# Order of loads, stores, first weight sums and last stores around the two ends of a mixing and routing kernel

## Chip, cores and metric

One core of a Trainium2 chip runs the whole kernel. The metric is the device time of one execution in microseconds (us), as the median of several runs. The engines are TensorE (PE, matmuls), VectorE (DVE), ScalarE (ACT), GpSimd (POOL) and SyncE (SP). Each has its own instruction stream; SP, ACT and POOL also issue DMAs, each on its own queue, in the order of the stream. An instruction that must wait holds up all that stands behind it in the same stream.

## The reference

```python
# x: 8 batches of 2496 tokens with 256 channels; 8 experts, F = 1024
X = np.fft.rfft(x, axis=1)                     # along the tokens
y = np.fft.irfft(X * (filt_r + 1j * filt_i), n=x.shape[1], axis=1)
x = y.reshape(8 * 2496, 256)
expert_idx = token_ids * np.int64(2654435761) % np.int64(8)
for e in range(8):
    mask = expert_idx == e
    h = np.maximum(x[mask] @ w1[e], 0.0)
    out[mask] = h @ w2[e]
```

All is float32. First the tokens of a batch are mixed by a filter in the frequency domain, then each mixed row goes through the two layers of the expert that its token's hash names.

## The kernel before

**Mixing.** The transform over 2496 = 39 x 64 tokens is done by matmuls with small tables in stages: stage 1 (`pa`), a turn or a trip through DRAM, forward (`pb`, then the filter's products `y` and `z` on DVE), back (`pc`), a second turn or trip, and stage 3 (`pd`), whose result `o` is copied out of PSUM. Batches 0 and 1 (`first`, `second`) are done on the chip alone, in the head, with transposes on PE between the stages. Batches 2 to 7 go through DRAM: stage 1 writes `mid` to d (batch 2's such stores are collected in a list, `put_off`, and issued together later), `load2` reads `mid` back, `load4` reads `t` back after the second trip. `load1` loads x, in three parts v = 0, 1, 2.

**Sorting.** In the head, the hashes of all tokens are counted on PE, DVE and POOL (`count`, `route`, `later`), which gives each token its row in a DRAM array `xs` that is sorted by expert into tiles of 256 tokens. POOL scatters every mixed row there by indirect DMA (L413): 44 scatters for batches 0 and 1.

**Experts.** 85 tiles are laid out; 80 always run, and up to 5 more in three nested conditional blocks at the end, by a count that is read at run time. With these inputs no conditional block is entered. A tile i loads its rows (`load`: four parts `xg` and a part `no` with the rows' numbers, L799), has them transposed (`token_parts`, DVE, L810), and multiplies by w1 (`up`, L842) and w2 (`down`, L877). Both layers of a tile use one level of Strassen's scheme: sums of the tile's blocks (`token_sums`, DVE, `st`, L823) and of the weights' blocks (`weight_sums`, `tw`, L832: four subtractions of 128x512, each of two SBUF operands) save products. `weight_sums(0)` runs on DVE, those of later tiles on POOL, one tile ahead. Tiles from 50 on use a second form (`both`) for both layers. `store` (L970) scatters the two halves of a tile's output rows `osb` to the output by indirect DMA on POOL. `weights(i + 2, k)` loads w1 or w2 of the tile after next on SP's queue.

**What sets the order.** A list `todo` holds pairs of a time and a piece of work. Pieces with a negative time run before tile 0, in the order of their times. The others are merged into the tiles: `run_until(t)` issues all with a time below t, and within tile i it is called before `down` with i + .6, in `down` after each of the first three quarters with i + .7, i + .8 and i + .9, and after `down` with i + 1. `spaced(a, b, n)` gives n times from a to b. So the stages of batches 2 to 7 are woven into the tiles, and each engine executes its part of this one order. Tiles are in stages by the batches whose rows they need: tiles 0 to 9 hold rows of batches 0 and 1 alone, and `load(10)` needs batch 2's too.

**Around the change.** The lines are those of the kernel before.

- Head, SP's queue: the first batch's x, the tables of part 1 (`load_tables(1)`: a part of the d-table and of the filter), then the second batch's x (`second.load1`, v = 0, 1, 2), each behind other tables (L470 to L486, L238).
- `begin()` (time -84.9) closes the pools of the head, opens those of the tiles (`gath`, `work`, `outs`, `nums`, `tpool`) and issues `load(0)` and `load(1)`, all ten parts on SP's queue. They wait for the last scatter of batch 1.
- Behind them on SP's queue: batch 3's x, parts 0 and 1 (times -75.3, -75.2), and batch 2's `mid` (`load2`, -75 to -74.7). On ACT's queue: the `put_off` stores (-75.5; L749).
- After the pieces, `token_parts(0)`, `token_sums(0)` and `weight_sums(0, nc.vector)` stand in this order on DVE; POOL's `weight_sums(1)` is the first of tile 0's step.
- `part2(2, ...)` and `part3(2, ...)` give the times of batch 2's forward, back and stage 3 and of their loads: the first `pb` is due at .5, in tile 0.
- At the end, after tile 79: `store(79)`, then `token_parts` of tiles 80 to 84 into spare parts of `mid`, and `load(82)` to `load(84)` on ACT's queue, then the conditional blocks (`rest`).

Of the kernel before, what the change touches and what calls it, by code (L numbers as in the profile page):

```python
# [11 lines left out]
F32 = mybir.dt.float32  # L12
# [7 lines left out]
P = 128  # L20
B, S, C = 8, 2496, 256
# [98 lines left out]
def kernel(  # L120
# [55 lines left out]
    def slot(kind):  # L176
# [8 lines left out]
                   for k in range(2)],  # L185
            "st": [spare[:, FP * C + 512 * k:FP * C + 512 * k + 512].rearrange("p (k t) -> p k t", k=4)
                   for k in range(2, 4)],
            "one": spare[:, FP * C + 2048:FP * C + 2048 + P]}

    def minus(eng, out_, a, b, op=OP.subtract):  # L190
        eng.tensor_tensor(out_, a, b, op=op)
# [278 lines left out]
    def load_tables(part):  # L470
        if part < 2:

            nc.gpsimd.tensor_copy(junk[:], first.x[2 * part][0:1, 0, 0:1])
        sl = S_PARTS[part]
        nc.sync.dma_start(out=d_t[:, sl, :], in_=d_dram.ap()[:, sl, :])
        for k in range(2):
            load_filter(k, sl)
# [250 lines left out]
                step(batches[j // (NS // 2)], j % (NS // 2))  # L728


    todo = [(t, lambda k=k: load_tables(k)) for k, t in enumerate((-160, -159, -157, -156))]
    todo += [(t, lambda v=v: second.load1(v)) for v, t in enumerate((-158, -156.5, -156.4))]
    todo += [(t, lambda u=u: first.stage1_c(u)) for u, t in enumerate(spaced(-155, -151, NU))]
    todo += [(-154.2, count), (-152, route), (-150.9, later)]
    todo += [(-137.2, places), (-128, tile_experts), (-121, experts), (-90, blanks)]
# [10 lines left out]
    todo += [(t, lambda v=v: batches[2].load1(v)) for v, t in enumerate((-119, -117.5, -116))]  # L746
    todo += [(t, lambda u=u: batches[2].stage1(u)) for u, t in enumerate((-101.5, -99.5, -84.8, -84.7, -84.6, -84.5))]

    todo += [(-75.5, lambda: [nc.scalar.dma_start(out=dram, in_=chip) for dram, chip in put_off])]  # L749
    todo += [(t, lambda k=k: weights(k // 2, k % 2)) for k, t in enumerate((-101, -98, -95, -92))]  # L750
    todo += [(-84.9, lambda: begin())]

    def batch(b, t1, t2, t3):

# [6 lines left out]
        return out  # L761

    todo += [(-75 + .1 * g, lambda g=g: batches[2].load2(g)) for g in range(4)]
    todo += [(-75.3 + .1 * v, lambda v=v: batches[3].load1(v)) for v in range(2)]
    todo += part2(2, spaced(.5, 3, N_2), [None] * 4 + [1], .6)
    todo += part3(2, spaced(4.3, 7.3, NU), [3.4, 3.6, 4.5]) + part1(3, spaced(1, 4, NU), [None, None, 2])
    todo += part2(3, spaced(6.4, 10, N_2), [5.2, 5.4, 5.6, 6.5, 7.5], .6)
    todo += part3(3, spaced(12, 16, NU), [11.2, 11.4, 12.5])
    todo += batch(4, (7.5, 11), (12.4, 16.4), (18.3, 22.3)) + batch(5, (13, 17), (18.4, 21.6), (23.2, 26.8))
# [6 lines left out]
    main = [t for t in todo if t[0] >= 0]  # L776


    gath = work = outs = nums = tpool = None
    xg, to_rows, parts, sums, rows = {}, {}, {}, {}, {}  # L780

    def begin():
        nonlocal gath, work, outs, nums, tpool
        rctx.close()
        gath, work, outs = pool(ctx, "gath", 2), pool(ctx, "work", 1), pool(ctx, "outs", 2)
        nums, tpool = pool(ctx, "nums", 8), pool(ctx, "tp", 2)
        for i in range(2):
            load(i)

    def load(i):  # L790

        g = gath.tile([P, TB // 32, C // 4], F32, name=f"xg_{i}", tag="xg")
        no = nums.tile([P, 2], I32, name=f"no_{i}", tag="no")
        rows = xs[tiles[i] * TB:(tiles[i] + 1) * TB, :]
        moves = [(g[32 * q:32 * q + 32, :, :], rows[:, 64 * q:64 * q + 64].rearrange("(a t) c -> t a c", t=32))
                 for q in range(4)]
        moves.append((no[:].bitcast(F32), rows[:, C:C + 1].rearrange("(h p) c -> p (h c)", p=P)))
        for to, src in moves:
            ld = (nc.sync if i < 2 else nc.scalar).dma_start(out=to, in_=src)  # L799
            for b in range(STAGES[stage_of[i]], B):  # L800
                tc.declare_no_dep(ld.ins, group=f"xs_{b}", reason="the tiles of a stage hold tokens of its batches alone")
            if stage_of[i] < G - 1:
                tc.declare_no_dep(ld.ins, group="xs_pad", reason="places without a token lie in the last stage alone")
            tc.add_to_no_dep_group("xs_read", ld.ins)
        xg[i], to_rows[i] = g, no
# [78 lines left out]
    def both(i, ht):  # L884

        w1, w2 = ws[i][0:2]
        x, st, t = parts[i], parts[i]["sums"], sums[i]
        t2, s, one = late["t2"][i % 2], late["sums"], late["one"]
        h11, h12, h21, h22 = [ht[:, h, 4 * f:4 * f + 4, :] for h in range(2) for f in range(2)]
        b11, b12, b21, b22 = [w2[:, 4 * f:4 * f + 4, P * c:P * c + P] for f in range(2) for c in range(2)]  # L890
        half = F // 2

        def bank(k, name):
            p, tag = (banks[k], k) if k in banks else (fps, "f")
            return p.tile([P, 4, P], F32, name=f"{name}_{i}", tag=tag)

        def product(ps, w, xx, first):
            for f in range(4):
                nc.tensor.matmul(out=ps[:, f, :], lhsT=w[:, f * P:(f + 1) * P], rhs=xx,  # L899
                                 start=first and f == 0, stop=True, skip_group_check=True)  # L900

        def second(ps, a, b, first):
            for f in range(4):
                nc.tensor.matmul(out=ps[:, 0, :], lhsT=a[:, f, :], rhs=b[:, f, :],  # L904
                                 start=first and f == 0, stop=True, skip_group_check=True)

        def relu(out, in_):
            nc.scalar.activation(out=out, in_=in_, func=AF.Relu)  # L908

        def plus(out, ps, other):  # L910
            nc.vector.tensor_tensor(out, ps, other, op=OP.add)  # L911

        a, b, c = [bank(k, "up" + k) for k in "abc"]
        g, e = bank("f", "upg"), bank("f", "upe")
        if i + 1 < NSURE:
            token_parts(i + 1, late["xt"][i % 2])
        product(a, w1[:, 0, 0:half], x[0, 0], True)
        nc.scalar.copy(out=h21, in_=a[:])
        if i + 2 < NT:
            load(i + 2)  # L920
        product(b, t[1], st[:, 1, :], True)
        plus(h12, b[:], h21)
        product(g, t[2], st[:, 2, :], True)
        plus(h21, g[:], h12)
        product(c, t[0], st[:, 0, :], True)
        plus(h22, c[:], h21)
        relu(h22, h22)
        product(e, t[3], x[1, 1], True)
        plus(h21, e[:], h21)
        relu(h21, h21)  # L930
        product(a, w1[:, 1, 0:half], x[0, 1], False)
        relu(h11, a[:])
        minus(nc.vector, s[:, 0], h21, h22, OP.add)
        product(c, w1[:, 1, half:], st[:, 3, :], False)
        plus(h12, c[:], h12)
        relu(h12, h12)
        weights(i + 2, 0)

        e, a = bank("b", "dne"), bank("d", "dna")
        b, c = bank("f", "dnb"), bank("f", "dnc")  # L940
        rows[i] = outs.tile([P, 2, C], F32, name=f"osb_{i}", tag="osb")
        o11, o12, o21, o22 = [rows[i][:, h, P * k:P * k + P] for h in range(2) for k in range(2)]
        second(e, h22, t2[:, 3], True)
        second(c, s[:, 0], t2[:, 0], True)
        second(a, h11, b11, True)
        nc.scalar.copy(out=one, in_=a[:, 0, :])
        minus(nc.vector, s[:, 1], s[:, 0], h11)
        minus(nc.vector, s[:, 2], h11, h21)
        minus(nc.vector, s[:, 3], h12, s[:, 1])
        second(b, s[:, 1], t2[:, 1], True)  # L950
        if i + 1 < NSURE:
            token_sums(i + 1, late["st"][i % 2], range(2))
        plus(o22, c[:, 0, :], one)
        plus(o21, e[:, 0, :], one)
        plus(o12, b[:, 0, :], one)
        second(a, h12, b21, False)
        nc.scalar.copy(out=o11, in_=a[:, 0, :])
        if i + 1 < NSURE:
            token_sums(i + 1, None, range(2, 4))
        second(b, s[:, 2], t2[:, 2], False)  # L960
        plus(o22, b[:, 0, :], o22)
        plus(o21, b[:, 0, :], o21)
        second(c, s[:, 3], b22, False)
        plus(o12, c[:, 0, :], o12)
        weights(i + 2, 1)
# [11 lines left out]
        piece()  # L977
    token_parts(0)
    token_sums(0)
    weight_sums(0, nc.vector)  # L980
    used = []

    def run_until(t):
# [32 lines left out]
            used.append(nc.values_load(used_i[0:1, 0:1], min_val=0, max_val=NT))  # L1016
        step(i)
    assert not main
    store(NSURE - 1)

    for i in range(NSURE, NT):
        token_parts(i, mid[:, i - NSURE, 0:2 * TB].rearrange("p (d h t) -> p d h t", d=DP, h=2))
        if i + 2 < NT:
            load(i + 2)
    blocks = [range(NSURE, NSURE + 1), range(NSURE + 1, NSURE + 2), range(NSURE + 2, NT)]

    def rest(k):
        with tc.If(used[0] > blocks[k][0]):
            for i in blocks[k]:
                ht = work.tile([P, 2, FP, P], F32, name=f"ht_{i}", tag="ht")  # L1030
                token_sums(i)
                weight_sums(i, nc.vector)
                up(i, ht)
                weights(i + 2, 0)
                down(i, ht)
                store(i)
                weights(i + 2, 1)
            if k + 1 < len(blocks):
                rest(k + 1)

    rest(0)

# [1 line left out]
_INS = ['x', 'filt_r', 'filt_i', 'moe_token_ids', 'moe_w1', 'moe_w2']  # L1044
# [24 lines left out]
```

## Time and profile before

| what | us |
|---|---|
| median of 3 runs (1466.46 to 1475.76) | 1469.89 |
| the profiled execution | 1478.73 |
| its span (first to last recorded event) | 1477.0 |
| PE busy in it | 1386.2 |
| DVE busy | 890.2 |
| POOL busy | 822.2 |
| ACT busy | 417.0 |
| HBM read and written over the span | 254 GB/s |

The profile is taken of one execution, whose time lies 8.84 us above the median. A line of the timeline gives the start, the busy time, the engine (PEld is the load of a matmul's stationary operand, SPq and ACTq are DMAs that the engine issues), the line of the kernel, the operation, `out<-in` by the program's names and how many of them follow each other without a break; in brackets stands the idle time of the engine before them and what ended it. In the page's second part the span is cut into 40 equal slices of 36.9 us, and a digit is the busy share in tenths.

| stretch | from, to (us) | what runs |
|---|---|---|
| head, first batch's x under way | 0 to 8.39 | tables, ids; PE idle |
| head, batches 0 and 1 and batch 2's stage 1 | 8.39 to 138.8 | PE, DVE and ACT mixing; scatters from 79.27 |
| seam | 138.8 to 154.7 | last scatters, batch 2's stores, first rows |
| tile 0 | 154.72 to 180.95 | first products, two `pb` groups |
| tiles 1 to 79 | 180.95 to 1463.7 | experts, batches 2 to 7 among them |
| end | 1463.7 to 1477.0 | last store, loads and transposes for tiles 80 to 84 |

### The profile page before, as it was taken

The page shows a single profiled execution, that of the slowest core. Times are in us where ns is not written, and L with a number is a line of the kernel's source. Part 1 is how long each engine was busy: PE and PEld are TensorE (multiplying, and loading weights), DVE is VectorE, ACT ScalarE, POOL GpSimd, SP SyncE. Part 2 cuts the span into 40 slices and gives each one's busy share as a digit, 9 for nine tenths or more (in the row PEclk, how much of TensorE's full clock was granted, in tenths as well). Part 3 has the DMA queues.
Part 4 walks back from the last instruction along what each step waited for, and adds up shares of the span by engine and source line. Part 5 has one row for each costly group of instructions (what it writes and reads, how often), then busy time and mean ns, then how long its engine had stood idle before and what let it go on. Part 6 is the DMA issues. An engine that isn't in the chain of part 4 may idle for free.

```text
span 1477.0 us, 26433 instructions
## 1 busy us (share of the span) xinstructions
PE 1386.2 (94%) x9466; PEld 1285.2 (87%) x9466; DVE 890.2 (60%) x1644; ACT 417.0 (28%) x770; POOL 822.2 (56%) x732
## 2 busy tenths in 40 slices
PE   6996699989999979999989999999999999999996
PEld 6984688879988868888978999999999999999996
DVE  6872466366465547534754468744656677777775
ACT  3553032223223213323222322222222222222221
POOL 5065323663475456558533487878855555555552
PEclk9999699999999989999999999999999999999998
DMA  8248466756897597688754667597751616161612
GB/s 218 56 131 251 144 196 186 215 167 208 260 272 232 182 279 247 193 272 274 256 155 130 193 212 249 182 268 240 232 183 45 213 44 211 44 211 41 209 41 55
DMA packets 245027, 273.10 MB, mean 185 GB/s; under 512 B 129020, under 2 KB 214959, under 8 KB 235469
## 3 DMA queue, kind: packets, MB, share of 16 engines
q1 hardware_dynamic: 87991, 168.19, 35.9%
q10 hardware_dynamic: 136982, 58.59, 16.0%
q0 software_dynamic: 19920, 44.59, 8.7%
q8 instruction: 77, 1.26, 0.3%
q14 instruction: 57, 0.47, 0.1%
HBM read 291.03 MB, written 83.53 MB: 254 GB/s over the span
## 4 chain that ended last, share of the span: by engine, by line
PE 59%; DMA 8%; DVE 1%; ACTq 1%; ACT 1%; issue 1%; SPq 0%; DVEq 0%
PE dps L877 16%; PE up_b L842 5%; PE dnc L904 4%; PE dna L904 4%; PE dnb L904 4%; DMA t<-d 3%; PE upa L899 3%; PE upc L899 3%; PE up_a L842 3%; DMA xg<-xs 3%; PE up_c L842 3%; PE pd L256 2%; PE pc L323 2%; PE pb L300 2%; PE upe L899 2%; PE upg L899 2%
## 5 line engine op out<-in xcount | busy, mean ns | idle before, releaser
L877 PE MATMUL dps<-wts,ht 128*128 128x256 f32 x1600 | 378.5, 388 | 27.6 <-ACT ht L846 27.6
L877 PEld LDWEIGHTS dps<-wts,ht 128*128 128x128 f32 x1600 | 307.2, 194 | 76.9 <-ACT ht L846 32.5
L970 POOL DMA_INDIRECT out_dram<-osb,no x160 | 167.1, 1044 | 261.9 <-DVE osb L911 142.8
L413 POOL DMA_INDIRECT xs<-o,sidx x176 | 176.5, 1003 | 175.1 <-issue 73.6
L832 POOL TENSOR_TENSOR tw<-wts 128x512 f32<-128x512 f32 x158 | 203.7, 1290 | 109.6 <-DMA wts<-in_moe_w_dram 79.4
L832 POOL TENSOR_TENSOR tw<-wts,tw 128x512 f32<-128x512 f32 x158 | 205.8, 1302 | 6.2
L849 DVE TENSOR_TENSOR ht<-up_b,ht 128x512 f32<-128x512 f32 x150 | 103.7, 691 | 112.0 <-PE up_b L842 102.3
L846 ACT ACTIVATE ht<-ht 128x512 f32<-128x512 f32 x150 | 92.0, 627 | 233.2 <-DMA xg<-xs 92.5
L310 DVE TENSOR_TENSOR z<-pb,filt 64x512 f32<-64x512 f32 x160 | 110.2, 689 | 36.4 <-PE pc L323 34.5
L842 PE MATMUL up_a<-xt,wts 128*128 128x128 f32 x800 | 115.6, 278 | 16.1 <-DVE xt L810 16.1
L882 DVE COPY osb<-dps 128x512 f32<-128x512 f32 x50 | 34.6, 692 | 155.0 <-PE dps L877 154.4
L842 PEld LDWEIGHTS up_a<-xt,wts 128*128 128x128 f32 x800 | 106.3, 194 | 19.6 <-POOL tw L832 16.5
L842 PE MATMUL up_b<-st,tw 128*128 128x128 f32 x800 | 107.6, 278 | 3.1 <-DVE ht L849 1.4
L842 PEld LDWEIGHTS up_b<-st,tw 128*128 128x128 f32 x800 | 98.5, 194 | 4.6 <-issue 2.5
L306 DVE TENSOR_TENSOR y<-pb,filt 128x512 f32<-128x512 f32 x80 | 55.2, 690 | 67.7 <-PE pb L300 65.8
L849 DVE TENSOR_TENSOR ht<-up_c,ht 128x512 f32<-128x512 f32 x100 | 69.1, 691 | 38.8 <-PE up_c L842 33.4
L908 ACT ACTIVATE ht<-ht 128x512 f32<-128x512 f32 x90 | 56.8, 631 | 121.4 <-DVE ht L911 76.0
L853 ACT COPY ht<-up_a 128x512 f32<-128x512 f32 x50 | 29.3, 586 | 175.4 <-PE up_a L842 160.1
L256 PE MATMUL pd<-t,wi_t 120*117 120x256 f32 x320 | 76.1, 380 | 1.3 <-DVE t L386 1.3
L326 ACT COPY mid<-pc 128x512 f32<-128x512 f32 x60 | 35.1, 585 | 146.5 <-PE pc L323 146.4
L311 DVE TENSOR_TENSOR y<-y,z 128x512 f32<-128x512 f32 x80 | 72.5, 907 | 2.7
L258 ACT COPY o<-pd 117x512 f32<-117x512 f32 x80 | 45.5, 586 | 99.3 <-PE pd L256 76.6
(203 smaller groups left out, 2482.1 us busy)
## 6 DMA issues: line engine op xcount, KB each, us to landing
wts<-in_moe_w_dram SPq DMA_DIRECT2D x160, 1024.0 KB
xg<-xs ACTq DMA_DIRECT2D x332, 64.0 KB
mid<-d SPq DMA_DIRECT2D x60, 256.0 KB
d<-mid ACTq DMA_DIRECT2D x60, 256.0 KB
d_t<-t2s SPq DMA_DIRECT2D x15, 1024.0 KB
e_t<-t2s SPq DMA_DIRECT2D x15, 1024.0 KB
d<-mid ACTq DMA_DIRECT2D x12, 960.0 KB
t<-d SPq DMA_DIRECT2D x12, 960.0 KB
```

Source lines behind the costliest of these rows:

```text
L256: nc.tensor.matmul(out=ps[0:cols * H, k, :], lhsT=w[:], rhs=src[:, 2 * i + k, :], start=True, stop=True)
L310: nc.vector.tensor_tensor(out=z[b], in0=ps[a], in1=f_t[1][64 * hi:64 * hi + 64, s1:s1 + 2, :], op=OP.mult)
L311: nc.vector.tensor_tensor(out=y[:], in0=y[:], in1=z[:], op=OP.add)
L413: st = nc.gpsimd.indirect_dma_start(out=xs[:], out_offset=bass.IndirectOffsetOnAxis(ap=index, axis=0), in_=rows, in_offset=None, bounds_ch ...
L832: eng.tensor_tensor(t[k][:], p, q, op=OP.subtract)
L842: nc.tensor.matmul(out=ps[bank][:, f, :], lhsT=w[:, f * P:(f + 1) * P], rhs=xx, start=first and f == 0, stop=True, skip_group_check=True)
L846: nc.scalar.activation(out=out, in_=in_, func=AF.Relu)
L849: nc.vector.tensor_tensor(out, ps[bank][:], other, op=OP.add)
L877: nc.tensor.matmul(out=ps[:, h, :], lhsT=ht[:, h, fp, :], rhs=w2[:, fp, :], start=(fp == 0), stop=(fp == FP - 1))
L899: nc.tensor.matmul(out=ps[:, f, :], lhsT=w[:, f * P:(f + 1) * P], rhs=xx, start=first and f == 0, stop=True, skip_group_check=True)
L904: nc.tensor.matmul(out=ps[:, 0, :], lhsT=a[:, f, :], rhs=b[:, f, :], start=first and f == 0, stop=True, skip_group_check=True)
L970: st = nc.gpsimd.indirect_dma_start(out=out[:], out_offset=bass.IndirectOffsetOnAxis(ap=to_rows[i][:, h:h + 1], axis=0), in_=o[:, h, :], i ...
```

## The change

Several edits stand in one diff. In the head: 14 matmuls of the identity with itself into a PSUM tile that nothing reads (`warm`); the first part of the second batch's x goes ahead of `load_tables(1)`; the `put_off` stores go from ACT's queue to SP's, where they stand behind the row loads and ahead of `load2`, and batch 3's x goes behind `load2`; `load(0)` and `load(1)` leave `begin` for a piece of their own, and of tile 0's five parts the last two are issued on ACT's queue; the pools of the tiles are opened in another order, and `weight_sums(0)` on DVE is issued in `begin`, ahead of tile 0's transpose. In the tiles: batch 2's forward, back and stage 3 get later times (the first `pb` at 1 instead of .5, the first `pd` at 4.6 instead of 4.3) and their loads too. At the end: tile 79's output rows get a buffer of their own in an idle part of the filter's tile (`late["last"]`), only tiles 80 and 81 are transposed ahead of the conditional blocks, the loads and transposes of tiles 82 to 84 move into the third block, and tile 79's store is issued behind the blocks, its second half first.

```diff
--- before.py
+++ after.py
@@ -185,7 +185,8 @@
                    for k in range(2)],
             "st": [spare[:, FP * C + 512 * k:FP * C + 512 * k + 512].rearrange("p (k t) -> p k t", k=4)
                    for k in range(2, 4)],
-            "one": spare[:, FP * C + 2048:FP * C + 2048 + P]}
+            "one": spare[:, FP * C + 2048:FP * C + 2048 + P],
+            "last": spare[:, FP * C + 2048 + P:FP * C + 2048 + P + 2 * C].rearrange("p (h c) -> p h c", h=2)}
 
     def minus(eng, out_, a, b, op=OP.subtract):
         eng.tensor_tensor(out_, a, b, op=op)
@@ -728,8 +729,15 @@
                 step(batches[j // (NS // 2)], j % (NS // 2))
 
 
-    todo = [(t, lambda k=k: load_tables(k)) for k, t in enumerate((-160, -159, -157, -156))]
-    todo += [(t, lambda v=v: second.load1(v)) for v, t in enumerate((-158, -156.5, -156.4))]
+    def warm(n):
+
+        ps = banks["a"].tile([P, 4, P], F32, name="warm", tag="a")
+        for k in range(n):
+            nc.tensor.matmul(out=ps[:, k % 4, :], lhsT=ident[:], rhs=ident[:], start=True, stop=True)
+
+    todo = [(-165, lambda: warm(14))]
+    todo += [(t, lambda k=k: load_tables(k)) for k, t in enumerate((-160, -159, -157, -156))]
+    todo += [(t, lambda v=v: second.load1(v)) for v, t in enumerate((-159.5, -156.5, -156.4))]
     todo += [(t, lambda u=u: first.stage1_c(u)) for u, t in enumerate(spaced(-155, -151, NU))]
     todo += [(-154.2, count), (-152, route), (-150.9, later)]
     todo += [(-137.2, places), (-128, tile_experts), (-121, experts), (-90, blanks)]
@@ -746,9 +754,9 @@
     todo += [(t, lambda v=v: batches[2].load1(v)) for v, t in enumerate((-119, -117.5, -116))]
     todo += [(t, lambda u=u: batches[2].stage1(u)) for u, t in enumerate((-101.5, -99.5, -84.8, -84.7, -84.6, -84.5))]
 
-    todo += [(-75.5, lambda: [nc.scalar.dma_start(out=dram, in_=chip) for dram, chip in put_off])]
+    todo += [(-75.5, lambda: [nc.sync.dma_start(out=dram, in_=chip) for dram, chip in put_off])]
     todo += [(t, lambda k=k: weights(k // 2, k % 2)) for k, t in enumerate((-101, -98, -95, -92))]
-    todo += [(-84.9, lambda: begin())]
+    todo += [(-84.9, lambda: begin()), (-84.4, lambda: [load(i) for i in range(2)])]
 
     def batch(b, t1, t2, t3):
 
@@ -761,9 +769,9 @@
         return out
 
     todo += [(-75 + .1 * g, lambda g=g: batches[2].load2(g)) for g in range(4)]
-    todo += [(-75.3 + .1 * v, lambda v=v: batches[3].load1(v)) for v in range(2)]
-    todo += part2(2, spaced(.5, 3, N_2), [None] * 4 + [1], .6)
-    todo += part3(2, spaced(4.3, 7.3, NU), [3.4, 3.6, 4.5]) + part1(3, spaced(1, 4, NU), [None, None, 2])
+    todo += [(-74.5 + .1 * v, lambda v=v: batches[3].load1(v)) for v in range(2)]
+    todo += part2(2, spaced(1, 3.5, N_2), [None] * 4 + [1.5], .6)
+    todo += part3(2, spaced(4.6, 7.5, NU), [4.0, 4.1, 4.8]) + part1(3, spaced(1, 4, NU), [None, None, 2])
     todo += part2(3, spaced(6.4, 10, N_2), [5.2, 5.4, 5.6, 6.5, 7.5], .6)
     todo += part3(3, spaced(12, 16, NU), [11.2, 11.4, 12.5])
     todo += batch(4, (7.5, 11), (12.4, 16.4), (18.3, 22.3)) + batch(5, (13, 17), (18.4, 21.6), (23.2, 26.8))
@@ -776,16 +784,16 @@
     main = [t for t in todo if t[0] >= 0]
 
 
+    sums = {}
     gath = work = outs = nums = tpool = None
-    xg, to_rows, parts, sums, rows = {}, {}, {}, {}, {}
+    xg, to_rows, parts, rows = {}, {}, {}, {}
 
     def begin():
         nonlocal gath, work, outs, nums, tpool
         rctx.close()
-        gath, work, outs = pool(ctx, "gath", 2), pool(ctx, "work", 1), pool(ctx, "outs", 2)
-        nums, tpool = pool(ctx, "nums", 8), pool(ctx, "tp", 2)
-        for i in range(2):
-            load(i)
+        tpool, nums, gath = pool(ctx, "tp", 2), pool(ctx, "nums", 8), pool(ctx, "gath", 2)
+        outs, work = pool(ctx, "outs", 2), pool(ctx, "work", 1)
+        weight_sums(0, nc.vector)
 
     def load(i):
 
@@ -795,8 +803,8 @@
         moves = [(g[32 * q:32 * q + 32, :, :], rows[:, 64 * q:64 * q + 64].rearrange("(a t) c -> t a c", t=32))
                  for q in range(4)]
         moves.append((no[:].bitcast(F32), rows[:, C:C + 1].rearrange("(h p) c -> p (h c)", p=P)))
-        for to, src in moves:
-            ld = (nc.sync if i < 2 else nc.scalar).dma_start(out=to, in_=src)
+        for k, (to, src) in enumerate(moves):
+            ld = (nc.sync if i < 2 and (i or k < 3) else nc.scalar).dma_start(out=to, in_=src)
             for b in range(STAGES[stage_of[i]], B):
                 tc.declare_no_dep(ld.ins, group=f"xs_{b}", reason="the tiles of a stage hold tokens of its batches alone")
             if stage_of[i] < G - 1:
@@ -938,7 +946,7 @@
 
         e, a = bank("b", "dne"), bank("d", "dna")
         b, c = bank("f", "dnb"), bank("f", "dnc")
-        rows[i] = outs.tile([P, 2, C], F32, name=f"osb_{i}", tag="osb")
+        rows[i] = outs.tile([P, 2, C], F32, name=f"osb_{i}", tag="osb") if i + 1 < NSURE else late["last"]
         o11, o12, o21, o22 = [rows[i][:, h, P * k:P * k + P] for h in range(2) for k in range(2)]
         second(e, h22, t2[:, 3], True)
         second(c, s[:, 0], t2[:, 0], True)
@@ -977,7 +985,6 @@
         piece()
     token_parts(0)
     token_sums(0)
-    weight_sums(0, nc.vector)
     used = []
 
     def run_until(t):
@@ -1016,18 +1023,20 @@
             used.append(nc.values_load(used_i[0:1, 0:1], min_val=0, max_val=NT))
         step(i)
     assert not main
-    store(NSURE - 1)
-
-    for i in range(NSURE, NT):
+
+    for i in range(NSURE, NSURE + 2):
         token_parts(i, mid[:, i - NSURE, 0:2 * TB].rearrange("p (d h t) -> p d h t", d=DP, h=2))
-        if i + 2 < NT:
-            load(i + 2)
     blocks = [range(NSURE, NSURE + 1), range(NSURE + 1, NSURE + 2), range(NSURE + 2, NT)]
 
     def rest(k):
         with tc.If(used[0] > blocks[k][0]):
             for i in blocks[k]:
                 ht = work.tile([P, 2, FP, P], F32, name=f"ht_{i}", tag="ht")
+                if i >= NSURE + 2:
+                    for j in ((i, i + 1) if i == NSURE + 2 else (i + 1,)):
+                        if j < NT:
+                            load(j)
+                    token_parts(i)
                 token_sums(i)
                 weight_sums(i, nc.vector)
                 up(i, ht)
@@ -1039,6 +1048,7 @@
                 rest(k + 1)
 
     rest(0)
+    store(NSURE - 1, (1, 0))
 
 # ---- launch: one core; inputs and outputs as the reference has them ----
 _INS = ['x', 'filt_r', 'filt_i', 'moe_token_ids', 'moe_w1', 'moe_w2']
```

## Prediction

> **What bounds the kernel now.** I read the page's engine table and slices first.
>
> ```profile
> PE 1386.2 (94%) x9466; PEld 1285.2 (87%) x9466; DVE 890.2 (60%) x1644; ACT 417.0 (28%) x770; POOL 822.2 (56%) x732
> PE   6996699989999979999989999999999999999996
> ```
>
> TensorE (PE) is busy 94% of the span. 1477.0 - 1386.2 leaves 90.8 us of idle time, so an edit that leaves PE's work alone can only win out of these, and out of matmuls run at half clock. The low slices are 0, 3, 4 (37 us each) and the last: the places that the diff touches. Next came the timelines there, head first:
>
> ```profile
> 30.72 3.74 PE L346 MATMUL pa<-wf_t,wts 117*128 117x120 f32 x16 [4.53 <-DMA wts<-in_x_dram]
> 38.10 1.94 PE L346 MATMUL pa<-wf_t,wts 117*128 117x120 f32 x16
> ```
>
> PE waits 4.53 us for the second batch's x, and then does 16 matmuls in 3.74 us which take 1.94 us later: the granted clock was 0.50 from 29.9 to 36.7. Then the seam between the head and the first tile, around T = 150.45, when the last scatter has landed and the first rows may be read:
>
> ```profile
> 143.07 0.90 POOL L413 DMA_INDIRECT xs<-o,sidx  x1 [0.31 <-issue]
> 150.50 1.81 SPq L799 DMA_DIRECT2D xg<-xs  x4
> ...
> 154.45 1.26 POOL L832 TENSOR_TENSOR tw<-wts,tw 128x512 f32<-128x512 f32 x1
> 154.66 1.20 DVE L823 TENSOR_TENSOR st<-xt 128x128 f32<-128x128 f32 x1
> ...
> 154.72 2.05 PE L842 MATMUL up_a<-xt,wts 128*128 128x128 f32 x8 [16.06 <-DVE xt L810]
> 155.41 9.67 SPq L238 DMA_DIRECT2D x<-in_x_dram  x6
> 155.89 0.29 DVE L823 TENSOR_TENSOR st<-st,xt 128x128 f32<-128x128 f32 x1
> ```
> ```profile
> 157.97 2.08 PE L842 MATMUL up_b<-st,tw 128*128 128x128 f32 x8 [1.20 <-DVE tw L832]
> 165.13 5.51 SPq L291 DMA_DIRECT2D mid<-d  x8
> 165.84 1.89 PE L877 MATMUL dps<-wts,ht 128*128 128x256 f32 x8
> 171.32 2.04 PE L300 MATMUL pb<-mid,d_t 128*128 128x256 f32 x4 [3.59 <-DMA mid<-d]
> 173.16 3.62 PE L877 MATMUL dps<-wts,ht 128*128 128x256 f32 x8
> ```
>
> The last scatter takes 7.4 us from issue to T; PE stands 16.06 us, and 3.59 us more for mid<-d in tile 0. The answer for the scatters gives their landing, in 139 to 150 and in 79 to 112:
>
> ```profile
> DMA to landing us min/median/max: 7.3/8.7/9.1
> DMA to landing us min/median/max: 2.6/2.8/4.6
> ```
>
> Between the two lies batch 2's stores on ACT's queue (issued 138.77 to 142.38); the DMA share was 0.88 from 140 to 148.5. Last the end:
>
> ```profile
> 1463.94 1.30 DVE L810 STREAM_TRANSPOSE mid<-xg 128x512 f32<-128x512 f32 x2
> 1466.08 0.98 POOL L970 DMA_INDIRECT out_dram<-osb,no  x1 [0.30 <-issue]
> 1474.10 0.71 DVE L810 STREAM_TRANSPOSE mid<-xg 128x512 f32<-128x512 f32 x1 [1.76 <-DMA xg<-xs]
> ```
>
> The last matmul ends at 1463.7; the span's last 13.3 us are the stores, and gathers and transposes for tiles that do not run.
>
> **The change, part by part.** Sums are against the profiled 1478.73 us (span 1477.0, 1.7 outside it), which is 8.8 above the median of 1469.89.
>
> *Warm-up and x (A).* The 14 matmuls run on an idle PE from about 1.4 us (ident is ready at 1.38). At the half-clock 0.23 us each (3.74/16) they end by 4.6; x lands at 8.39, so they cost nothing, and 3.8 us of idle follow. After 2.54 us of idle (258.37) the granted clock fell from 1.00 to 0.60 over the next 3 us, so I take the warm-up as lost; if it held, it would shorten the first matmuls, which need 4.5 us to 12.9, by 2.2. The Trainium skill ("TensorE: Matmul & The Clock Gate", "What's actually happening") has the clock fall only after an idle window of about 3.4 us, free-running; that would keep most warm-ups, as 3.8 us seldom hold a whole window, and A by it would be about -2. The row at 258.37, where less was enough, decides for me. Moving x's first part ahead of the 384 KB d-table and filter part takes the 4.53 away, but the bytes ahead of the last x part do not change: its last packet ends at 38.8 in the trace, and PE, done earlier with the first two parts, waits there instead, cold as before. I take -1, bounds 0 and -3.2 (the stall less 1.3).
>
> *Stores off the scatters (B).* They go to SP's queue behind the row loads, which wait for the last scatter. The scatter then lands like those of 79 to 112: 143.07 + 2.6 to 4.6, say 146.1 for T'. -4.4, bounds -2.8 to -4.8.
>
> *First weight sums ahead of the rows (C).* In the built order DVE's four sums of tile 0 wait for the last scatter as POOL's for tile 1 do (a pool that reuses memory), so both start at T'. DVE's 4 x 0.69 would end at T'+2.9, before the rows land at T'+3.46; up_b would start when up_a, at T'+4.3, has run its 2.05: T'+6.3 against T+7.5 now, -1.2. But see the 1.20 above: an add of two SBUF operands that takes 0.28 alone ended 0.15 after POOL's sum did, and its neighbours took 0.29 once POOL was done. Of L311's 128x512 adds, the 15 beside a POOL sum average 1.72, against 0.72 for 44 alone. 4 x 1.72 = 6.9: xt waits on DVE until T'+7.1, is done at 7.8, up_a ends at 9.85, and up_b starts there: +2.3. If the two alternate, 4 x (0.69 + 1.26) = 7.8: +3.3. I take +2.3. The skill ("SBUF — State Buffer", "SBUF: two separate sides") says that a DVE operation with two SBUF inputs and a GpSimd operation that reads SBUF exclude each other for a whole instruction; that is the alternating case, and would make C +3.3. POOL's own four sums, 5.0 alone, end by T'+8, and tile 1 needs them 15 us later.
>
> *Batch 2's second stage half a tile later (D).* Tile 0 from its first dps to tile 1's up_a took 180.95 - 165.84 = 15.1 us: 32 dps and two pb groups, with 3.59 of idle and 3.4 us at half clock behind it. Now it holds 32 dps, 4 x 1.73 = 6.9; the two pb groups cost 2 x 0.87 = 1.7 in tile 1. 15.1 - 8.6: -6.5, bounds -4 and -7. Its cover is SP's queue: row loads to T'+4.5, three stores whose data are long ready, then mid<-d, which waits until they land (9.7 us after issue in the trace: T'+15), 5.5 of issue and about 1.5 of landing: T'+22. The first pb is due after tile 0 (T'+9.9+7.9+6.9 = 24.7) and tile 1's sums (7.2 here, 180.95 to 188.1): T'+32. Batch 3's x follows at T'+20 to 30, and behind it w1 of tile 2, issued at T+22.7 now, at T'+30 then; it lands 5 us later (186.60 to POOL's 191.55), and POOL needs it near T'+43. So 8 to 10 us of cover.
>
> *Later tiles (E).* Batch 2's t_2 parts are loaded behind w1 of tile 6 (5.7 us into tile 4) and the first pd comes behind 24 of tile 4's dps, 7.9 + 5.2 = 13.1 us in: 7.4 us of room. In the chain t<-d took from 7.78 to 16.48 us. So 0 to 9 of stall, and 1.7 for a cold clock: 0 to +10.7; two of the four rows lie close to the room, the two long ones far later, and I take +1.5.
>
> *End (F).* The 15 loads (ACT) and three transposes move into a block that is not entered; tile 79's store follows POOL's branch, which costs nothing since POOL idles 11.44 us before it. DVE ends with its two transposes near 1465.2 instead of 1474.81. POOL remains: stores to 1466.4 (its wait on the osb stays), then its closing drain, which took 5.13 us here (1471.06 to 1476.19), then 0.8: 1472.3, -4.7. If the drain must wait for the landing (4.1 after the last store began, 1470.2): 1476, -1; if it is short, as it was only waiting for DVE's queue: 1469.5, -7.5. I take -5, since the store starts up to 0.7 earlier without the semaphore step that sat before it.
>
> Sum: -1 - 4.4 + 2.3 - 6.5 + 1.5 - 5 = -13.1. From 1478.73 that is 1465.6, and from the median 1469.89 - 13.1 = 1456.8.
>
> **Rivals.** (1) *Everything holds* (C without contention, A -3.2, E 0, F -7.5): -3.2 - 4.4 - 1.2 - 6.5 - 7.5 = -22.8, 1447. For: x is early, DVE's sums might be done before POOL's start. Against: both wait for one event. (2) *The seam gives back what it gains*: A 0, B -2.8, C +3.3, D -4, E +6, F -1 give +1.5, 1471: no change. For: SP's queue and t<-d are as long as their cover. (3) *Slower*: SP's queue blocked by the stores. If store and mid<-d take longer than their 25 us at T'+5 to 30, w1 of tile 2 comes late; beyond 8 us each further one stands still on PE, so 21 us more are needed to eat 13.1. At 30 more (the queue twice as slow) it is 30 - 8 - 13.1 = +9, and a half clock of 3.4 us and tile 3's weights behind it make it about +16, 1486. For: the scatters' landing trebled beside those stores. Against: some 5.5 MB at the 318 GB/s of 166 to 171.3 need 17 us.
>
> **How the numbers follow.** Forecast 0.62, (1) 0.18, (2) 0.14, (3) 0.06. One per cent, 14.7 us, is about what a measurement of this kernel can tell from no change. The forecast is within 1.6 us of it: a third of it (0.20) falls beyond, all of (1) too: faster 0.38. Within 1%: 0.42 + 0.14 = 0.56. Slower 0.06. The range runs from (1)'s 1447 to (2)'s 1471.
>
> **What would show it.** A scatter that lands 3 us after 143; tw on DVE at 1.2 to 2 us apiece, and up_a later than T'+7; no pb in tile 0 and tile 1's up_a near T'+25 against T+30.5; the last 13.3 us cut to 8. I am wrong if w1 of tile 2, mid<-d or t<-d stops PE in tiles 1 to 5, or if the closing drain stays where it was.

## The result, and the profile after

The changed kernel took 1462.92 us (median of 20 runs, 1455.12 to 1469.09) against 1476.76 for the kernel before beside it (20 runs, 1466.46 to 1482.28): a ratio of 0.9911, with a 95% interval of 0.9891 to 0.9931. That is 13.1 us of the 1469.89 from which the forecast started, and 13.1 us were forecast. The agreement is better than its parts: two of the six terms were wrong, in opposite directions, so that the total came out right by luck.

The profiled execution took 1457.74 us (span 1455.8), 5.2 below the median, while that of before lay 2.0 above the median of its 20 runs. So the two profiles differ by 21.0 us, some 7 more than the medians. The runs of one kernel spread over 14 to 16 us; places are read from the profiles here, and the size of the whole from the medians.

From the page, PE's share and slices:

```profile
PE 1385.8 (95%) x9494; PEld 1285.8 (88%) x9494; DVE 896.2 (62%) x1641; ACT 417.2 (29%) x770; POOL 823.4 (57%) x732
...
PE   8996798999999979999989999999999999999997
```

PE's work is the same, and idle time has gone: 1455.8 - 1385.8 = 70.0 us against 90.8. The first slice rose from 6 to 8, but slices 3 and 4 only from 6, 6 to 6, 7: most of the seam's wait is still there (13.19 us before up_a, 16.06 then). PE's timeline of the head:

```profile
1.44 6.08 PE L736 MATMUL warm<-ident 128*128 128x128 f32 x28 [1.44 <-POOL sign L506]
8.02 3.80 PE L347 MATMUL pa<-wf_t,wts 117*128 117x120 f32 x32 [0.50 <-DMA wts<-in_x_dram]
...
14.28 9.51 PE L347 MATMUL pa<-wf_t,wts 117*128 117x120 f32 x56 [2.10 <-issue]
...
28.02 1.94 PE L347 MATMUL pa<-wf_t,wts 117*128 117x120 f32 x16
...
39.62 2.26 PE L347 MATMUL pa<-wf_t,x 117*128 117x120 f32 x16 [2.12 <-DMA x<-in_x_dram]
```

The warm-up lasts until x lands, the first 32 pa take 3.80 us where they took 5.93, the wait of 4.53 us near 26 is gone and 2.12 us stand before the last part of x. A new wait of 2.10 us stands ahead of the next 56 pa; the granted clock was 0.50 from 14 to 20, and these pa took 9.51 us (6.42 in most of the runs below). The seam, from the timeline of all engines:

```profile
141.22 0.89 POOL L414 DMA_INDIRECT xs<-o,sidx  x1 [0.30 <-issue]
143.51 3.30 SPq L807 DMA_DIRECT2D xg<-xs  x7
...
143.68 0.69 DVE L840 TENSOR_TENSOR tw<-wts 128x512 f32<-128x512 f32 x1 [11.13 <-DMA xs<-o,sidx]
143.76 1.73 POOL L840 TENSOR_TENSOR tw<-wts 128x512 f32<-128x512 f32 x1 [1.65 <-DMA xs<-o,sidx]
...
144.41 1.63 DVE L840 TENSOR_TENSOR tw<-wts,tw 128x512 f32<-128x512 f32 x1
145.57 1.59 POOL L840 TENSOR_TENSOR tw<-wts,tw 128x512 f32<-128x512 f32 x1
145.97 1.75 DVE L840 TENSOR_TENSOR tw<-wts 128x512 f32<-128x512 f32 x1
...
147.41 9.17 SPq L757 DMA_DIRECT2D d<-mid  x3
...
150.06 2.08 PE L850 MATMUL up_a<-xt,wts 128*128 128x128 f32 x8 [13.19 <-DVE xt L818]
...
151.92 1.91 PE L850 MATMUL up_b<-st,tw 128*128 128x128 f32 x8
...
157.83 6.01 SPq L292 DMA_DIRECT2D mid<-d  x8
...
158.22 7.07 PE L885 MATMUL dps<-wts,ht 128*128 128x256 f32 x32
...
165.13 1.05 PE L850 MATMUL up_a<-xt,wts 128*128 128x128 f32 x8
...
165.76 9.40 SPq L239 DMA_DIRECT2D x<-in_x_dram  x6
...
176.00 1.96 PE L257 MATMUL pa<-x,wf_t 117*120 117x256 f32 x8 [3.58 <-DMA x<-in_x_dram]
```

The row loads are issued 2.3 us after the last scatter instead of 7.4, and 7.0 us sooner on the clock. DVE's sums take up to 1.75 us, turn about with POOL's. Tile 0 runs its 32 dps without a break. Tile 1 starts 21.6 us after the row loads (30.5 before), but its first pa waits 3.58 us for batch 3's x. Two more new waits stand in tiles 3 and 4 (PE's timeline):

```profile
232.26 1.93 PE L301 MATMUL pb<-mid,d_t 128*128 128x256 f32 x4 [3.69 <-DVE z L311]
...
259.20 1.99 PE L257 MATMUL pd<-t,wi_t 120*117 120x256 f32 x8 [1.66 <-DMA t<-d]
```

Tile 8 starts 13.7 us sooner than before and the last matmul ends 16.0 us sooner (1447.65 against 1463.70). From there to the end of the span it is 8.15 us instead of 13.30:

```profile
1447.89 1.29 DVE L818 STREAM_TRANSPOSE mid<-xg 128x512 f32<-128x512 f32 x2
1448.84 0.97 POOL L978 DMA_INDIRECT out_dram<-filt,no  x1 [0.31 <-issue]
```

### The profile page after: what moved, and what is told of

Same layout as the page of the kernel before. It is cut to its first block, busy times and chain, and to the rows that moved or that the text cites. A ratio compares the mean times of both kernels' runs of the same rounds, so it can differ in the third digit from the quotient of the medians.

```text
span 1455.8 us, 26473 instructions
## 1 busy us (share of the span) xinstructions
PE 1385.8 (95%) x9494; PEld 1285.8 (88%) x9494; DVE 896.2 (62%) x1641; ACT 417.2 (29%) x770; POOL 823.4 (57%) x732
## 4 chain that ended last, share of the span: by engine, by line
PE 82%; DMA 10%; DVE 3%; issue 1%; ACT 1%; ACTq 1%; SPq 0%; POOL 0%; POOLq 0%; DVEq 0%
PE dps L885 23%; PE up_b L850 7%; PE up_a L850 5%; PE up_c L850 5%; PE pb L301 4%; PE pd L257 4%; PE dnc L912 4%; PE dna L912 4%; PE dnb L912 4%; PE upc L907 3%; PE upa L907 3%; PE pc L324 3%; PE pa L257 3%; DMA xg<-xs 2%; PE upe L907 2%; PE upb L907 2%
## 5 line engine op out<-in xcount | busy, mean ns | idle before, releaser
L885 PE MATMUL dps<-wts,ht 128*128 128x256 f32 x1600 | 373.6, 384 | 17.5 <-ACT ht L854 17.4
L850 PEld LDWEIGHTS up_a<-xt,wts 128*128 128x128 f32 x800 | 105.9, 193 | 16.6 <-DVE xt L818 13.7
```

Source lines behind the costliest of these rows:

```text
L850: nc.tensor.matmul(out=ps[bank][:, f, :], lhsT=w[:, f * P:(f + 1) * P], rhs=xx, start=first and f == 0, stop=True, skip_group_check=True)
L885: nc.tensor.matmul(out=ps[:, h, :], lhsT=ht[:, h, fp, :], rhs=w2[:, fp, :], start=(fp == 0), stop=(fp == FP - 1))
```

## The experiments

Twelve runs, four on each of three chips: e1 to e4, e5 to e8, e9 to e12. The kernel before was timed beside them (medians 1498.64, 1498.91 and 1477.0 us), so only ratios are compared across chips. The changed kernel itself ran beside e9 to e12 only. All edits are to the changed kernel unless said.

**The end alone, and all but the end.** `e1_end_alone` is the kernel before with the last three hunks of the diff and the buffer that they need; `e2_without_end` is the changed kernel with those hunks taken back.

> The kernel before with only the end of the change: tile 79's rows in their own buffer, tiles 82 to 84 loaded and transposed inside the third conditional block, tile 79's store behind the blocks. Theory of the forecast (the end is a term of its own, worth 5 us): from the last matmul to the end of the span 8.2 us as in the changed kernel, against 13.3 before; ratio 0.9966. Rival (most of the gain lies at the end, as what the head wins is given back in the tiles): ratio near 0.992, with the same 8.2 us.

> The changed kernel with the end of the kernel before. Theory (head, seam and tile 0 are worth about 8 us by the forecast's terms): ratio to the kernel before 0.9945, from the last matmul to the end of the span 13.3 us. Rival (given back in the tiles): ratio 0.998 to 1.000. Second rival (the two profiles are right as they stand, 16 us up to the last matmul): ratio 0.989.

Measured: e1 0.9967 (0.9945 to 0.9990, 12 runs), with 8.1 us from the last matmul to the end; e2 0.9957 (0.9936 to 0.9977, 12 runs), with 12.9 us. 0.9967 x 0.9957 = 0.9924: the two parts add up to the whole within its interval. The end gives about 4.9 us (1.5 to 8.1 by its interval), the rest about 6.3 (3.4 to 9.4). The rival by which the end is nearly everything falls, and so does the one that takes the profiles at their word (0.989).

The head and seam of e1 are those of the kernel before, but its timeline of the seam is not the one from which the forecast started:

```profile
149.20 0.89 POOL L414 DMA_INDIRECT xs<-o,sidx  x1 [0.30 <-issue]
...
151.69 1.81 SPq L800 DMA_DIRECT2D xg<-xs  x4
...
155.91 0.59 ACTq L750 DMA_DIRECT2D d<-mid  x1
```

Here ACT was still copying batch 2's stage 1 results and came to the stores only at 155.91, behind the row loads; the last scatter took 2.5 us, not 7.4. So stores on ACT's queue meet the last scatters in one execution and not in another (on another chip), and where they don't, there is nothing to win from moving them.

**First weight sums behind the rows again.**

```diff
-        weight_sums(0, nc.vector)          # in begin()
...
     token_sums(0)
+    weight_sums(0, nc.vector)
```

> The changed kernel with the first weight sums on DVE behind the transpose and the token sums again, as before. Theory (the move costs time, since DVE's sums run beside POOL's): xt at about T + 3.5 as the rows land, up_a at T + 4.3, up_b at T + 7.5 as in the kernel before, 0.9 sooner than the T + 8.46 of the changed kernel, and the first sums on DVE at 0.69 each. Rival (the move is a gain, the sums being done while the rows land): up_b later than T + 8.46. The whole time moves by less than its noise by either.

Measured: 0.9915 (0.9882 to 0.9947), no difference from 0.9911. up_a started 4.1 us after the row loads' issue and up_b 7.6 after, as predicted; in the changed kernel it was 6.6 and 8.4. The move costs 0.8 us at up_b, and the whole does not show it.

**POOL's sums held back.**

```diff
+        if i == 0:
+            nc.gpsimd.tensor_copy(late["one"][0:1, 0:1], sums[0][3][0:1, 0:1])
         if i + 1 < NSURE:
             weight_sums(i + 1)
```

> The changed kernel, with POOL's four sums for tile 1 held back until DVE's four for tile 0 are done (a one-element copy on POOL reads DVE's last result). Theory (two engines' sums of SBUF operands stand in each other's way): DVE's four take 0.69 each, 2.8 in all instead of 5.7, xt starts as the rows land near T + 3.5, up_a at T + 4.3, up_b near T + 6.4: 2 us sooner than in the changed kernel. Rival (DVE's sums were stretched by the DMA traffic, not by POOL): they still take 1.6 to 1.75 each and up_b stays at T + 8.4.

Measured: 0.9926 (0.9894 to 0.9957). From its timeline:

```profile
149.14 0.69 DVE L840 TENSOR_TENSOR tw<-wts,tw 128x512 f32<-128x512 f32 x1
...
149.75 0.68 DVE L840 TENSOR_TENSOR tw<-wts 128x512 f32<-128x512 f32 x1
...
150.35 0.69 DVE L840 TENSOR_TENSOR tw<-wts,tw 128x512 f32<-128x512 f32 x1
...
151.16 0.18 POOL L1008 COPY filt<-tw 1x1 f32<-1x1 f32 x1 [4.32 <-DVE tw L840]
...
151.87 0.34 ACTq L807 DMA_DIRECT2D xg<-xs  x1
...
154.08 0.71 DVE L818 STREAM_TRANSPOSE xt<-xg 128x512 f32<-128x512 f32 x1 [3.04 <-DMA xg<-xs]
```

With POOL out of the way each sum takes 0.69: it was POOL that stretched them. But up_b came 8.5 us after the row loads all the same: ACT, still copying batch 2's last results, issued its part of the rows 3.6 us late, and xt waited for that. In e2 it was 4.5 us late, and up_a started 12.0 us after the row loads (6.6 in the changed kernel, where ACT issued it at once). The forecast has no term for this part of the change.

**Stores back on ACT's queue.**

```diff
-    todo += [(-75.5, lambda: [nc.sync.dma_start(out=dram, in_=chip) for dram, chip in put_off])]
+    todo += [(-84.45, lambda: [nc.scalar.dma_start(out=dram, in_=chip) for dram, chip in put_off])]
```

> The changed kernel with batch 2's three stores on ACT's queue again, ahead of the row loads, as in the kernel before. Theory (the stores' traffic holds up the last scatters): the last scatter takes 7 to 9 us from issue to the row loads instead of 2.3, so T comes 4 to 5 us later; mid<-d no longer waits on SP for the stores, so mid<-d and batch 3's x come sooner against T and the wait of the first pa in tile 1 (3.6 us in the changed kernel) goes. Ratio near 0.994, between the changed kernel's 0.991 and 0.9957. Rival (the early T came from the head before it, not from the stores): the last scatter still lands within 3 us.

Measured: 0.9964 (0.9939 to 0.9990). From its timeline:

```profile
143.00 0.89 POOL L414 DMA_INDIRECT xs<-o,sidx  x1 [0.30 <-issue]
...
145.29 11.95 SPq L807 DMA_DIRECT2D xg<-xs  x7
...
149.70 2.56 ACTq L757 DMA_DIRECT2D d<-mid  x2
...
152.66 1.50 ACTq L807 DMA_DIRECT2D xg<-xs  x1
...
158.65 0.71 DVE L818 STREAM_TRANSPOSE xt<-xg 128x512 f32<-128x512 f32 x1 [7.47 <-DMA xg<-xs]
```

A miss in the place. ACT came to the stores at 149.02, behind the last scatter, which took 2.3 us to the row loads; the stores met the row loads instead: seven issues took 11.95 us instead of 3.30, and ACT's own part of the rows stood behind the stores. xt began 13.4 us after the row loads, against 5.8. So the run does not test whether the stores hold up the scatters. It shows that stores beside the row loads cost about 8 us (0.9964 against 0.9911, on different chips); how much of that comes of the part on ACT's queue, which the kernel before does not have, was not tried.

**No warm-up; x later.** `e6_no_warm` drops `warm(14)`; `e7_x_later` puts the time -159.5 back to -158.

> The changed kernel without the 14 matmuls on the identity. Forecast's theory (they cool down before x lands and are worth nothing): the first 32 pa in 3.8 us all the same, cnt_ps near 11.7. Rival (they last until x lands, as the trace shows them at 1.44 to 7.5, and keep the clock): the first 32 pa take 5.9 us as before, cnt_ps L548 runs near 14 and what DVE does behind it starts 2 to 2.5 us later; T moves by 0 to 2 us, as PE waits for x's last part at 37 in any case.

> The changed kernel with the second batch's first x part behind load_tables(1) again, as before. Forecast's theory: PE's 4.2 to 4.5 us wait for x near 26 us is back, with 16 pa at half clock behind it; the wait for x's last part near 37 is gone; T comes 1 us later. Rival (the order of x is worth the whole stall): T comes 3 to 5 us later.

Measured: e6 0.9933 (0.9910 to 0.9957), e7 0.9980 (0.9960 to 1.0000). Without warm-up the first 32 pa took 6.01 us and cnt_ps ran at 14.60 instead of 11.66, yet the first scatter came at 74.80, within the 73.69 to 76.55 of the nine other experiments with the early x (78.16 in the profile of the changed kernel). Much of the gain is lost at once: the next pa start at 14.97 without warm-up and at 12.8 to 14.3 with it, behind a wait of up to 2.10 us. The ratios, 0.9933 and 0.9911, do not tell the two kernels apart. With the late x PE waited 6.79 us, ran at half speed behind it, and the first scatter came at 80.03, the row loads at 154.5 against 144.9 to 148.4 in the five experiments that have the early x and the warm-up on the first two chips:

```profile
31.91 3.74 PE L347 MATMUL pa<-wf_t,wts 117*128 117x120 f32 x16 [6.79 <-DMA wts<-in_x_dram]
```

By these runs the place of one load is worth 3 to 6 us at the first scatter and 6 to 10 at the seam, and about 10 us of the whole (0.9980 against 0.9911, on different chips), more than the rival had. On one chip, e1 against e2, e3 and e4 gives less for x and warm-up together: 3.2 to 5.1 us at the first scatter and 3.4 to 6.8 at the row loads.

**Batch 2's second half early again.**

```diff
-    todo += part2(2, spaced(1, 3.5, N_2), [None] * 4 + [1.5], .6)
-    todo += part3(2, spaced(4.6, 7.5, NU), [4.0, 4.1, 4.8]) + ...
+    todo += part2(2, spaced(.5, 3, N_2), [None] * 4 + [1], .6)
+    todo += part3(2, spaced(4.3, 7.3, NU), [3.4, 3.6, 4.5]) + ...
```

> The changed kernel with batch 2's second half at the times of the kernel before: two pb groups in tile 0, the first pd due at 4.3, loads of t_2 at 3.4, 3.6, 4.5. Theory (the delay is what the later stores need): mid<-d lands near T + 21, the first pb in tile 0 is due near T + 16.5, so PE waits 4 to 6 us there and runs at half clock for 3.4 us; tile 1 starts near T + 30 instead of T + 21.7, the wait for batch 3's x in tile 1 is gone, and the ratio is 0.995. Rival (what is late in tile 0 is won in tiles 1 to 5, the order being better there): ratio 0.991 as the changed kernel.

Measured: 0.9879 (0.9846 to 0.9911), better than the changed kernel's own figure. It was run again beside the changed kernel, with two variants. `e11_x3_first` also moves batch 3's x from times -74.5, -74.4 to -75.3, -75.2; `e12_early_sp_pool` adds POOL's wait of e4 and puts all parts of tile 0's rows on SP.

> The changed kernel once more, beside the next three on one chip. All theories: ratio to the kernel before 0.989 to 0.994. It is the mark for the run with batch 2's earlier times.

> The changed kernel with batch 2's second half at the earlier times, as once before, now beside the changed kernel. Theory (the delay is a loss of its own: PE waits 3.6 us for batch 3's x in tile 1, 3.7 us behind DVE in tile 3 and about 2 us for t<-d in tile 4, against one wait of 1.7 us in tile 0): ratio 0.988, 4 to 5 us below the changed kernel, and tile 8 starts 4 to 8 us sooner after T. Rival (the forecast's: the delay is worth 6.5 us, and the last run was a lucky one): ratio 0.994 or above.

> The changed kernel with batch 2's second half at the earlier times, and batch 3's x ahead of mid<-d on SP's queue as in the kernel before. Theory (what ends the wait in tile 0 is the order of these loads on SP, not the delay): x's six loads take 9 us of the queue, mid<-d lands 9 us later, the first pb in tile 0 waits 8 to 11 us instead of 1.7 and half clock follows; ratio 0.994. Rival (the stores' landing sets the time of mid<-d, whatever stands between): the wait stays below 4 us, ratio 0.988.

> The changed kernel with batch 2's second half at the earlier times, POOL's sums for tile 1 held back until DVE's for tile 0 are done, and all five parts of tile 0's rows on SP's queue. Theory: DVE's sums take 2.8 us, the rows land near T + 3.5, up_a near T + 4.3 and up_b near T + 6.4, 2 us before the changed kernel; mid<-d comes no sooner, so the first pb's wait in tile 0 grows from 1.7 to 3 us or more and takes most of it back; ratio 0.987. Rival (no further gain behind that wait): ratio 0.988 to 0.989.

Measured on one chip: e9 0.9909 (0.9883 to 0.9935), e10 0.9864 (0.9834 to 0.9893), e11 0.9932 (0.9900 to 0.9963), e12 0.9862 (0.9834 to 0.9889). e10 lies 5.3 us below e9 (1457.96 against 1463.30). The two intervals overlap a little, but the earlier run pointed the same way. From the timelines, SP's loads and the first pb in tile 0, of e10 and then of e11:

```profile
144.97 9.20 SPq L757 DMA_DIRECT2D d<-mid  x3
...
155.44 5.00 SPq L292 DMA_DIRECT2D mid<-d  x8
...
159.33 1.10 PE L301 MATMUL pb<-mid,d_t 128*128 128x256 f32 x4 [1.65 <-DMA mid<-d]
```
```profile
142.07 9.09 SPq L757 DMA_DIRECT2D d<-mid  x3
...
151.26 4.84 SPq L239 DMA_DIRECT2D x<-in_x_dram  x6
...
156.21 6.25 SPq L292 DMA_DIRECT2D mid<-d  x8
...
163.24 2.05 PE L301 MATMUL pb<-mid,d_t 128*128 128x256 f32 x4 [8.89 <-DMA mid<-d]
```

With mid<-d right behind the stores, pb in tile 0 waits 1.65 us and the clock stays up; with batch 3's x between, 8.89 us. So the order on the queue took the wait away, not the delay. (In e1, with the order of before, the same wait was 7.52.) e9 shows the delay's price again: waits of 3.56 for x, 3.69 behind DVE and 1.97 for t<-d, against 1.65 and one of 2.46 for ACT in e10. Tile 8 started 180.3 us after the row loads in e9 and 171.1 in e10; in these two executions later tiles took back 6.3 of the 9.2. In e12 the four sums took 2.8 us, but POOL's, now later, stretched the token sums instead, and up_b came 7.2 us after the row loads: nothing won over e10.

e10 and e12 beat both kernels: 19 us below the kernel before on that chip (1477.0), the best version found.

## Why the prediction was right, and where it was not

- **A, warm-up and x, -1.** Wrong in two places. "They end by 4.6" counted one matmul for each call; the trace lists two for a 128x128 product of this type (x28 for 14), 6.08 us, so only 0.50 us were left in which to cool. That error had no weight that e6 could show. The other had: that PE "waits there instead, cold as before" for x's last part. It waited 1.0 to 2.1 us there where the trace names that wait, mostly without half clock behind it, in place of 4.53 and 6.8 us at half clock, and the pa behind it started at 36.6 to 39.6, against 42.27 before. The bound of -3.2 was too narrow: on one chip the first scatter came at 73.74 to 75.69 (e2, e3, e4) against 78.88 in e1, whose head is that of before, and e7 puts the whole of it higher still. In the two profiles of the result it came only 1.1 us sooner (78.16 against 79.27), the changed kernel's having run at half clock from 14 to 20. A price that the term left out: in nine runs PE waits 0.97 to 1.26 us near 28 for the d-table, which now stands behind x.
- **B, stores, -4.4.** In the two profiles of the result the mechanism held: 2.3 us from the last scatter to the row loads, 7.4 before, so -5.1. The term left out that the stores need not meet the last scatters (2.5 us in e1) and that row loads suffer like scatters (e5). And it is not these stores alone that make scatters late: in the kernel before, scatters issued from 119 to 125 took 10.4 to 12.7 us to land, ahead of the stores, at a DMA share of 0.99. So how much of the measured total is B's is not shown.
- **C, weight sums, +2.3.** The mechanism was right and shown by e4; the size too high. Four sums took 5.7 us instead of 6.9, DVE having won the first turn, and up_b stood 8.4 us after the row loads against 7.5: +0.9. The trace agrees with the exclusive turns that the Trainium skill states ("SBUF — State Buffer", "SBUF: two separate sides"): the three that came after a sum of POOL's ended 0.55 or 0.56 us behind it.
- **D, batch 2 later, -6.5.** This step failed. Of the 3.59 us that it was to remove, the order of SP's queue alone leaves 1.65, with no half clock (e10), and the delay itself, beside that order, loses about 5 us (e10 against e9). "So 8 to 10 us of cover" held for mid<-d and w1, but it did not count batch 3's x: tile 1 came 3 us sooner than the sum had it, x's loads took SP until 175.2, and the first pa waited 3.58.
- **E, later tiles, +1.5.** t<-d made PE wait 1.66 and 1.97 us in tile 4, as sized, though the prediction also names that as a sign of being wrong; the 3.69 us behind DVE in tile 3 were not foreseen.
- **F, end, -5.** Held: -4.9 in e1. From the end of POOL's last store instruction (1449.81) to the end of the span it was 6.0 us, as the drain's 5.13 and 0.8 had it.

All but the end was forecast at -8.1 and measured at -6.3 (e2). The right total came of an x worth more than was granted and a delay that costs instead of winning; that the two errors cancelled was luck. The single parts do not add up to the whole: undoing x costs 10, the stores 8 and the end 5 us, and undoing the delay wins 5, which makes 18 and not 13. A late head may be partly hidden behind the stores and the other way round, but no run takes both back, and e5's stores stand elsewhere than in the kernel before.

What stays open: what the stores' move is worth alone, and that sum; why tiles 3 and 4 wait in the delayed order alone was read from the waits, not tried; and which of e12's two additions undoes the other.

## What to carry over

Credit a removed wait to one edit only, and undo the edits one at a time against the changed kernel: here two edits aimed at one wait, and beside the first the second was a loss. When a load is moved ahead, work out anew when PE reaches the next load, at full clock; do not carry the old wait over. Work that is made later to hide a queue also brings forward what stood behind it, so the cover of every other load on that queue has to be counted again. And look at more than one execution before a meeting of two transfers becomes a term: ACT came to the same stores at 138.77 in one and at 155.91 in another.

## What the runs showed of the hardware

The clock record cannot be trusted at the start: the page's windows grant 1.00 from 0 to 17 us in the kernel before, while the first 32 pa took 5.93 us there and 3.80 behind 6 us of matmuls. DMA traffic in flight makes small transfers late: in the kernel before, scatters landed after 2.6 to 4.6 us from 79 to 112 and after 10.4 to 12.7 from 119 to 125, where the DMA share was 0.99. And the head varies by itself: in ten profiled executions with the early x and the warm-up the first scatter came at 73.7 to 78.2 us, and the row loads at 138.2 to 148.4, over all chips.
